# Skip term of five output sums moved from TensorE to ScalarE and GpSimd, last output sum in two halves

## The chip, the cores and the metric

One NeuronCore of a Trainium2 chip runs the whole program. The metric is device time in microseconds (us) of one execution. Before the change three runs took 287.53, 287.78 and 289.35 us, median 287.78 us. The profiled execution took 285.57 us, of which 283.8 us are the span from the first to the last instruction; the other 1.8 us lie around it.

## The reference

Two branches are computed from the same kind of input and blended by a gate for each token. Branch A is an attention with memory, 32 heads, in four segments of 512 tokens. Branch B is a state space convolution of the input, done as a long FFT, plus the input times a skip vector.

```
x = A_x
g = _sigmoid((x * gate_w).sum(-1, keepdims=True))
a = _A_ref(x, ...)          # heads' outputs o, then o @ wo
b = _B_ref(...)             # y, then y + u * Dskip
return g * a + (1 - g) * b
```

The output is 2048 x 512 in bf16. In the kernel the token is split as 16 p + b4, where p is a partition, so the output is made as 16 sums of 128 x 512, one for each b4 from 0 to 15. Every one of them is (1 - g) times a bracket of four parts: the attention output through wo (four 128-deep products, the factor g/(1 - g) put into the heads' outputs before), the convolution's two halves (one product each), and the skip term x * Dskip.

## The kernel before, in words

Nothing is scheduled while the program runs. Every operation is recorded by `op` with its engine and its dependencies; the table `ORDER` then fixes the order of all operations, the engine of those that either ScalarE or VectorE can do, and the slot of each buffer or PSUM bank. `replay` walks that table and `emit` writes five in-order instruction streams (PE, ACT, DVE, POOL, SP), where an instruction waits only on semaphores of what it depends on. All DMAs of the part that matters here are issued by SP, one behind the other: a DMA that waits for a buffer holds all DMAs behind it.

`conv` treats 32 units u. Names used below: `Ku` (a product on PE and its eviction), `Yu` (a product on VectorE), `Vu` (a product on PE, its eviction into a buffer of the pool V, and a DMA that spreads it into V2, whose second half V2[1] comes from units 16 to 31). The last units that run are 31, 29 and 30. `X31` is a DMA that Y31 needs.

`finals` makes the 16 sums, spread by `ORDER` over the last 35 us among the last attention and convolution work. For sum b4 the steps are named

- `fin`: first products into a PSUM bank; `fir`: convolution half 0 (V2[0]);
- `fih`: the last wo product, which needs the last heads (`oT3.3`); `fis`: convolution half 1, which needs V2[1] and so the DMAs of units 25, 26, 29 and 30;
- `out`: eviction times (1 - g), held in `omg4T`, then a 256 KB store for two sums together.

Sums 0 to 7 are *spilled* (`SPILL`): after `fir` the bank is emptied by `spl` on VectorE into an f32 buffer Ab and taken again by `fih`. Ab holds the skip term already: `xD` on VectorE (L1528) makes x times (1 - g) times Dskip, from x rows loaded by `xr` (L1524), two sums to a load. Sums 8 to 15 are *held*: they keep their bank from `fin` to `out`, and their skip term is made by PE, four 128-wide products of x transposed with a diagonal matrix, at the start of `fin` (L1534). Their `out` is a plain scaled copy, on ScalarE (L232) or VectorE (L233).

A bank that an eviction empties is given to a later product; the PE instruction waits for that eviction. In the program before, `fin0` takes the bank of `K30` and `fin14` the bank of `V29`.

Of the kernel before, what the change touches and what calls it, by code (L numbers as in the profile page):

```python
# [358 lines left out]
def c_pe(mode, *ns):  # L359
    return ("P", mode, ns)  # L360
# [14 lines left out]
NWARM = 5  # L375
SPILL = {0: 1, 1: 1, 2: 1, 3: 1, 4: 2, 5: 2, 6: 0, 7: 0}
# [89 lines left out]
1687/0/1 1688a 1742 840 1682/0 1683/4/0 1006/2 1007 1776 1689/3 1008 1724/2 1727 1702/0 1703 1718/6 1690/1/3 1719
1026/5 1027v 1764/2 1765 1766 1780/5 1732/1 1657 1684a 1740/0 1743 1797/4 1685 1798 1777 1691a 1692 1799 1704 1800/0
1801v 1767/1 1733/1 1753/1 1721/0 1778/2 1769/7 1717/3 1720 1712/4 1713/3 1714 1722/4 1723 1768a 1779a 1728/2 1729
1770 1781 1782 1783 1784a 1734/6 1771 1772 1773v 1802/3 1803 1804 1785 1774 1754/5 1755 1735 1737/4 1730 1760/0 1761
1736 1705/5 1706 1707 1744/7 1745/2 1786/1 1762 1731 1715 1763 1805 1806a 1807 1787 1788 1789/1 1746 1738 1739 1791/6  # L470
1792 1790a 1793 1794 1747 1795a 1796
# [70 lines left out]
def build_graph(nc, es, A_x, A_wq, A_wk, A_wv, A_wo, A_beta, B_A_re, B_A_im, B_B_re, B_B_im,  # L542
# [147 lines left out]
    xrP = mkpool("xr", 2048, 2, 3)  # L690
# [819 lines left out]
    def finals(V2, k0):  # L1510
# [4 lines left out]
        for b4 in range(16):  # L1515
            held = b4 not in SPILL
            S.key = k0 + b4
            P = S.ps()
            Ab = None if held else Tile(AbPs[SPILL[b4]], F32)
            if not held:  # L1520
                if b4 % 2 == 0:
# [4 lines left out]
                    xr[b4] = xr[b4 + 1] = T  # L1526
                S.tag = "xD%d" % b4
                op("DVE", ("V1s", 512), lambda e, b4=b4, Ab=Ab, T=xr[b4]: e.scalar_tensor_tensor(  # L1528
                    ap(Ab, n=512), ap(T, (b4 % 2) * 512, n=512), ap(omg4T, b4, n=1), ap(DbT, n=512), ALU.mult, ALU.mult), r=[xr[b4], omg4T, DbT], w=[Ab], key=k0 - 10 + b4)
# [126 lines left out]
```

## Time and profile before

| | |
|---|---|
| median of the runs | 287.78 us (287.53 to 289.35) |
| profiled execution | 285.57 us; span 283.8 us |
| PE busy | 258.8 us, 91% |
| DVE busy | 265.0 us, 93% |
| ACT busy | 254.3 us, 90% |
| POOL busy | 5.0 us, 2% (memsets at the start and two later) |
| granted TensorE clock | 0.993 over the span |

The page names the line of the helper that emits an instruction: L713 is every product of PE but a few, L229 and L230 are plain evictions on ACT and DVE, L232 and L233 scaled ones, L225 every DMA. The trace is followed in us from the start of the span. A row of the timeline has start, length, engine, line, operation, shapes, count, and in brackets the idle time of the engine ahead of it and what ended it.

### The profile page before, as it was taken

The page shows a single profiled execution, that of the slowest core. Times are in us where ns is not written, and L with a number is a line of the kernel's source. Part 1 is how long each engine was busy: PE and PEld are TensorE (multiplying, and loading weights), DVE is VectorE, ACT ScalarE, POOL GpSimd, SP SyncE. Part 2 cuts the span into 40 slices and gives each one's busy share as a digit, 9 for nine tenths or more (in the row PEclk, how much of TensorE's full clock was granted, in tenths as well). Part 3 has the DMA queues.
Part 4 walks back from the last instruction along what each step waited for, and adds up shares of the span by engine and source line. Part 5 has one row for each costly group of instructions (what it writes and reads, how often), then busy time and mean ns, then how long its engine had stood idle before and what let it go on. Part 6 is the DMA issues. An engine that isn't in the chain of part 4 may idle for free.

```text
span 283.8 us, 9330 instructions
## 1 busy us (share of the span) xinstructions
PE 258.8 (91%) x3947; PEld 157.5 (56%) x3947; DVE 265.0 (93%) x617; ACT 254.3 (90%) x320; POOL 5.0 (2%) x10
## 2 busy tenths in 40 slices
PE   5778888887989899989999989999999999999995
PEld 2434454564656556756765657665555454556663
DVE  3999999999999999999999999999999999997774
ACT  5999999999999999999989999999999999994122
POOL 5000000000000000000000000000000000000000
PEclk9999899999999999999999999999999999999999
DMA  6997752422115346824743388588676786793415
GB/s 164 274 203 173 218 170 85 130 80 53 42 28 143 76 114 183 229 86 73 214 135 103 76 254 236 183 207 203 207 223 171 217 192 187 219 206 105 116 74 222
DMA packets 60187, 44.49 MB, mean 157 GB/s; under 512 B 36209, under 2 KB 53490, under 8 KB 60146
## 3 DMA queue, kind: packets, MB, share of 16 engines
q1 hardware_dynamic: 60146, 43.90, 57.4%
q8 instruction: 31, 0.51, 0.8%
q14 instruction: 10, 0.08, 0.1%
HBM read 22.09 MB, written 7.86 MB: 106 GB/s over the span
## 4 chain that ended last, share of the span: by engine, by line
ACT 43%; PE 41%; DVE 9%; issue 4%; DMA 2%; SPq 0%; ACTq 0%; DVEq 0%
PE psum L713 40%; ACT sb L1197 15%; ACT sb L229 13%; ACT sb L1244 8%; DVE sb L1353 3%; ACT sb L857 3%; ACT sb L865 2%; DVE sb L1362 1%; DVE sb L1356 1%; DMA scr_Z<-sb 1%; ACT sb L1028 1%; DMA sb<-c_ident 1%; ACT sb L1079 1%; DVE sb L1365 1%; ACT L935 0%
## 5 line engine op out<-in xcount | busy, mean ns | idle before, releaser
L713 PE MATMUL psum<-sb 128*128 128x17 bf16 (+18 forms) x3859 | 253.2, 230 | 16.4 <-ACT sb L1197 7.4
L713 PEld LDWEIGHTS psum<-sb 128*128 128x128 bf16 (+6 forms) x3859 | 152.3, 101 | 115.1 <-issue 19.3
L229 ACT ACTIVATE sb<-psum 128x512 bf16<-128x512 f32 (+4 forms) x155 | 87.7, 624 | 6.5 <-PE psum L713 5.8
L1244 ACT ACTIVATE sb<-psum 128x2048 bf16<-128x2048 f32 x40 | 75.9, 1899 | 2.2 <-PE psum L713 1.8
L1197 ACT ACTIVATE sb<-psum 128x2048 bf16<-128x2048 f32 (+1 forms) x40 | 70.0, 1751 | 2.3 <-PE psum L713 2.1
L1353 DVE TENSOR_TENSOR sb<-sb 128x4096 bf16<-128x4096 bf16 (+3 forms) x24 | 37.6, 1567 | 0.0
L230 DVE CAST sb<-psum 128x512 bf16<-128x512 f32 (+1 forms) x49 | 29.9, 625 | 1.2 <-PE psum L713 0.9
L1362 DVE TENSOR_TENSOR sb<-sb 128x512 bf16<-128x512 bf16 (+1 forms) x48 | 24.9, 534 | 0.1
L1256 DVE TENSOR_TENSOR sb<-sb 128x1024 bf16<-128x1024 bf16 (+1 forms) x40 | 22.5, 576 | 0.2
L1494 DVE TENSOR_TENSOR sb<-sb 128x1024 bf16<-128x1024 bf16 x32 | 21.5, 684 | 0.9 <-ACT sb L229 0.5
L1356 DVE TENSOR_TENSOR sb<-sb 128x2048 bf16<-128x2048 bf16 (+3 forms) x24 | 20.6, 859 | 0.0
L232 ACT ACTIVATE sb<-psum,sb 128x512 bf16<-128x512 f32 x6 | 4.0, 687 | 12.3 <-PE psum L713 12.3
L1161 DVE TENSOR_TENSOR sb<-psum,sb 128x256 bf16<-128x256 f32 x32 | 13.3, 415 | 0.3
L1365 DVE TENSOR_TENSOR sb<-sb 128x512 bf16<-128x512 bf16 (+1 forms) x24 | 12.7, 531 | 0.0
L857 ACT ACTIVATE sb<-sb 128x512 f32<-128x512 f32 x18 | 11.8, 659 | 0.0
L1158 DVE RECIPROCAL sb<-psum 128x16 f32<-128x16 f32 x32 | 7.8, 249 | 2.0 <-PE psum L713 1.8
L1298 DVE TENSOR_TENSOR sb<-psum,sb 128x512 bf16<-128x512 f32 x12 | 8.3, 689 | 0.2
L865 ACT ACTIVATE sb<-sb 128x512 bf16<-128x512 f32 x12 | 8.0, 683 | 0.0
L1079 ACT ACTIVATE sb<-sb 128x512 bf16<-128x512 bf16 x12 | 8.0, 662 | 0.0
L1028 ACT ACTIVATE sb<-psum 128x512 bf16<-128x512 bf16 x12 | 7.7, 645 | 0.0
L858 DVE TENSOR_TENSOR sb<-sb 128x256 f32<-128x256 f32 x18 | 7.4, 418 | 0.0
L859 DVE SCALAR_TENSOR_TENSOR sb<-sb 128x256 f32<-128x256 f32 x18 | 7.4, 417 | 0.0
(78 smaller groups left out, 121.8 us busy)
## 6 DMA issues: line engine op xcount, KB each, us to landing
sb<-sb SPq DMA_DIRECT2D x64, 128.0 KB, 3.2
sb<-c_DN SPq DMA_DIRECT2D x32, 224.0 KB, 3.1
scr_Z<-sb SPq DMA_DIRECT2D x16, 256.0 KB, 2.7
sb<-scr_Z SPq DMA_DIRECT2D x16, 256.0 KB, 3.7
sb<-in_A_x_dram SPq DMA_DIRECT2D x5, 512.0 KB, 4.7
sb<-c_DN SPq DMA_DIRECT2D x16, 160.0 KB, 3.4
out_dram<-sb SPq DMA_DIRECT2D x8, 256.0 KB, 2.0
scr_O<-sb SPq DMA_DIRECT2D x12, 128.0 KB, 3.1
```

The lines of the kernel that those rows point to most:

```text
L229: fa = lambda e: e.activation(dst(), src(), ACT.Copy)
L230: fd = lambda e: e.tensor_copy(dst(), src())
L713: mm = lambda e, o_, l, r_, st, sp, **kw: e.matmul(o_, lhsT=l, rhs=r_, start=st, stop=sp, skip_group_check=True, **kw)
L857: op("ACT", ("As", 512), lambda e, sq=sq, Z=Z: e.activation(ap(sq, n=512), ap(Z, n=512), ACT.Square), r=[Z], w=[sq], key=PW[h] + PWS * k)
L1197: o = op("ACT", ("Ax", 4 * n), lambda e: e.activation(ap(pT, dims=[[512, 4], [1, n]]), ap(P, dims=[[512, 4], [1, n]]), ACT.Exp, scale=0.25 ...
L1244: o = op("ACT", ("Ax", 2048), lambda e, P=P, pT=pT: e.activation(ap(pT, n=2048), ap(P, n=2048), ACT.Exp, scale=0.25), r=[P], w=[pT])
L1256: op("DVE", ("V2", 128 * nb), lambda e, pT=pT, dims=dims: e.tensor_tensor(ap(pT, dims=dims + [[1, 128]]), ap(pT, dims=dims + [[1, 128]]), ...
L1353: op("DVE", ("V2n1" if n == 1 else "V2", 512 * n), lambda e: e.tensor_tensor(ap(tile, 2 * dst, [[2 * (sp - dst), 2], [2 * ne, 128], [1, 2 ...
L1356: op("DVE", ("V2n1" if n == 1 else "V2", 256 * n), lambda e: e.tensor_tensor(D_(), D_(), ap(tile, 2 * sp + ne * 128, [[-ne * 128, 2], [2 * ...
L1362: op("DVE", ("V2x" if sstep > 2 else "V2", 256 * n), lambda e, half=half: e.tensor_tensor(run(t2, n, 0, 1) if half else run(tile, ne, dst, ...
L1365: op("DVE", ("V2", 256 * n), lambda e: e.tensor_tensor(D_(), D_(), ap(t2, n * 128, [[-n * 128, 2], [2 * n, 64], [1, 2 * n]]), ALU.add), r= ...
L1494: op("DVE", ("V2", 1024), lambda e, Y=Y, XAB=XAB, K3=K3, Ke=Ke, xo=xo, u=u: e.tensor_tensor(ap(Y, dims=[[512, 2], [1, 512]]), ap(XAB, xo, ...
```

## The change

For five held sums, `DSK` = 9, 14, 8, 10 and 11, `fin` no longer makes the skip term on PE. It is made into an f32 buffer, as for a spilled sum, and `out` becomes an operation of VectorE that adds it while it evicts. For nine sums, `GSK` = those five and the spilled ones 2, 3, 4 and 5, the skip buffer is made in two steps: `xS` on ScalarE (x times 1 - g) and `xM` on GpSimd (times Dskip, in place). Sums 0, 1, 6 and 7 keep `xD` on VectorE. The five held sums load their x rows by five new DMAs of 128 KB, `xq`. GpSimd gets a library load (an instruction printed as ISA) ahead of its first product.

Sum 13, the last one, is made in two halves of 256 columns in two banks; its first half is evicted by ScalarE, its second by VectorE (`outb13`). Sums 12 and 13 are stored apart, 128 KB each.

```diff
+DSK = (9, 14, 8, 10, 11,)
+GSK = (3, 14, 5, 8, 10, 2, 9, 11, 4,)
...
-1686/0 1671 1009/5 1013 1696/2 1759 1622 1697/6/3 1698a 1699 1664 1005 1016 1017 1018 1019/1 1741/7 1020 1021/1
+1662/4/2 1663a 1686/0 1815/0 1734/1 1671 1009/5 1013 1696/2 1763 1622 1768/1 1816/0 1817 1785/2 1776/3 1697/6/3 1698a
...
-    xrP = mkpool("xr", 2048, 2, 3)
+    xrP = mkpool('xr', 2048, 4, 3)
+    xqP = mkpool('xq', 1024, 4, 3)
...
+    AbhP = mkpool('Abh', 2048, 6, 3)
...
+            skip = held and b4 not in DSK
...
+            last = b4 == 13
+            P = [S.ps(), S.ps()] if last else [S.ps()]
...
+            elif not skip:
+                S.tag = "xq%d" % b4
+                T, xo = Tile(xqP, BF16), 0
+                S.dma(lambda T=T: ap(T, n=512), lambda b4=b4: bass.AP(x.tensor, x.offset + b4 * 512, [[8192, 128], [1, 512]]), 131072, w=[T])
+            if not skip and b4 in GSK:
+                S.tag = "xS%d" % b4
+                op("ACT", ("As", 512), lambda e, b4=b4, Ab=Ab, T=T, xo=xo: e.activation(
+                    ap(Ab, n=512), ap(T, xo, n=512), ACT.Copy, scale=ap(omg4T, b4, n=1)), r=[T, omg4T], w=[Ab])
+                S.tag = "xM%d" % b4
+                op("POOL", ("G", 512), lambda e, Ab=Ab: e.tensor_tensor(
+                    ap(Ab, n=512), ap(Ab, n=512), ap(DbT, n=512), ALU.mult), r=[DbT], w=[Ab])
...
-                if held:
+            def f1(e, P=P, b4=b4, skip=skip):
+                w = 512 // len(P)
+                if skip:
                     for kc in range(4):
...
+                    op("PE", c_pe("F", 256, 256), f4, r=o4 + [woT, G2T, V2[1]], pw=[Pj], acq=[ou])
...
+                    S.evac(lambda ou=ou, j=j, b4=b4: ap(ou, (b4 % 2) * 512 + 256 * j, n=256), lambda Pj=Pj: ap(Pj, n=256), 256,
+                           r=[Pj, omg4T], pw=[ohs[j], ou], scale=lambda b4=b4: ap(omg4T, b4, n=1))
...
+            elif skip:
+                S.evac(dst, lambda P=P: ap(P, n=512), 512, r=[P, omg4T], pw=[ohs[0], ou], scale=lambda b4=b4: ap(omg4T, b4, n=1))
             else:
...
+            if b4 in (12, 13):
```

The order of PE's operations is the same before and after; `fin` of the five sums is shorter. The orders of SP and ACT differ.

SP, about 249 to 265 us of the trace. In the program before (the rows are, in order: oT1.3, V28, X31, xr2, CD30, V27, V20, V31 and V26, oT2.3, xr4, V25):

```order
L1309 DMA_TRANSPOSE sb<-scr_O 128x1x512
L225 DMA sb<-sb 8x16x512 [waits q_ACT]
L225 DMA sb<-sb 64x1024
L225 DMA sb<-in_A_x_dram 128x1024 [waits q_DVE]
L225 DMA sb<-c_DN 128x896 [waits q_PE]
L225 DMA sb<-sb 8x16x512 [waits q_ACT]
L225 DMA sb<-sb 8x16x512
L225 DMA sb<-sb 8x16x512 [waits q_ACT]
L225 DMA sb<-sb 8x16x512
L1309 DMA_TRANSPOSE sb<-scr_O 128x1x512
L225 DMA sb<-in_A_x_dram 128x1024
L225 DMA sb<-sb 8x16x512
```

And now (oT1.3, xr2, V28, X31, CD30, xq14, xr4, V27, V20, then xq8, xq10 and xq9 in one row, V31, V26):

```order
L1317 DMA_TRANSPOSE sb<-scr_O 128x1x512
L225 DMA sb<-in_A_x_dram 128x1024 [waits q_DVE]
L225 DMA sb<-sb 8x16x512 [waits q_ACT]
L225 DMA sb<-sb 64x1024
L225 DMA sb<-c_DN 128x896 [waits q_PE]
L225 DMA sb<-in_A_x_dram 128x512
L225 DMA sb<-in_A_x_dram 128x1024 [waits q_DVE]
L225 DMA sb<-sb 8x16x512 [waits q_ACT]
L225 DMA sb<-sb 8x16x512
L225 DMA sb<-in_A_x_dram 128x512 x3
L225 DMA sb<-sb 8x16x512 [waits q_ACT]
L225 DMA sb<-sb 8x16x512
```

xr2 stands ahead of V28 and X31 now, and xr4 ahead of V27; both wait for VectorE, xr2 for the end of xD1 and xr4 for the end of xD7, whose buffers they take (the order's slots of the pool xr are the same two as before, though it has four). xq11 is issued behind V30.

ACT, from the last exponentials (L1244 before, L1252 now) to its end. Before (V27, sc3.3.B1, then V26, V31, K30, V29, V30, then the evictions out8, out10, out11, out15, out12, out13):

```order
L229 ACTIVATE sb<-psum 128x512 x2
L1244 ACTIVATE sb<-psum 128x2048
L229 ACTIVATE sb<-psum 128x512 x5
L232 ACTIVATE sb<-psum,sb 128x512 x6
L1610 UNCONDITIONAL_BRANCH
```

And now (K29 and V27, sc3.3.B1, xS3, V26, xS14, V31, xS5 and xS8, K30, xS10, V29, xS2, V30, then xS9, xS4 and xS11, out15 and out12, half of out13):

```order
L1252 ACTIVATE sb<-psum 128x2048
L1545 ACTIVATE sb<-sb 128x512
L229 ACTIVATE sb<-psum 128x512
L1545 ACTIVATE sb<-sb 128x512
L229 ACTIVATE sb<-psum 128x512
L1545 ACTIVATE sb<-sb 128x512 x2
L229 ACTIVATE sb<-psum 128x512
L1545 ACTIVATE sb<-sb 128x512
L229 ACTIVATE sb<-psum 128x512
L1545 ACTIVATE sb<-sb 128x512
L229 ACTIVATE sb<-psum 128x512
L1545 ACTIVATE sb<-sb 128x512 x3
```

The five evictions of the convolution have six steps `xS` between and ahead of them, each of which waits for its x rows or stands behind one that does; ACT's eviction of V31 waits, before and after, for the DMA of V27, whose buffer it takes. out8, out10 and out11 have gone to VectorE.

GpSimd, from its last memset to its end, which had only the branch there before (xM3, 14, 5, 8, 10, 2, 9, 11 and 4 in this order; the last one waits for nothing that the one ahead had not waited for):

```order
L1003 MEMSET sb 128x128 [waits q_PE] x2
L1548 ISA
L1548 TENSOR_TENSOR sb<-sb 128x512 [waits q_ACT] x8
L1548 TENSOR_TENSOR sb<-sb 128x512
L1658 UNCONDITIONAL_BRANCH
```

VectorE loses xD3, xD5, xD4 and xD2 and gains out8, out10, out11 and the 256-wide outb13 at its very end.

More of the change, by code (lines that the diff above doesn't have):

```diff
@@ L466 @@
[L466 to L470, printed above, removed]
@@ L1546, in finals @@
             S.tag = "fir%d" % b4
[L1547 removed]
+            op("PE", c_pe("F", 512), lambda e, P=P, fv=fv, held=held: [fv(e, Pj, j, 512 // len(P), q=0, stop=not held) for j, Pj in enumerate(P)][-1], r=[G2T, V2[0]], pw=P)
             if not held:
                 S.tag = "spl%d" % b4
[L1550 to L1552 removed]
```

83 lines of the change are left out of this document (54 added, 29 removed).

## The prediction

> **What bounds the kernel now.** I read the chain of waits first, from the end.
>
> ```profile
> 248.28 32.26 PE psum L713 x261
> 280.53 0.02 issue
> 280.56 0.69 ACT sb L232
> ```
>
> The last 32 us before the final eviction are one unbroken run of TensorE products. The stretches of the trace say the same of the place where the sums are made (columns: stretch, length, busy time and count of PE, clock, DMA share, GB/s).
>
> ```profile
> 254.20:280.53 26.33, 26.32 (x213) 1.00 0.39 122
> 270.51:273.53 3.02, 3.02 (x15) 1.00 0.00 0
> 266.08:266.33 0.25, 0.25 (x5) 1.00 0.38 107
> ```
>
> PE has no gap to lose: whatever leaves its stream there comes off the end, unless a wait takes its place. The second row gives the pace of 512-wide products, 3.02 us for 14 that start in it, 0.216 us each. The third is the stretch from the start of fin11's four skip products to the start of its first wo product: 0.25 us for the four.
>
> VectorE is the next busiest; its evictions at the end:
>
> ```profile
> 268.95 0.75 DVE L233 TENSOR_SCALAR sb<-psum,sb 128x512 bf16<-128x512 f32 x1 [1.19 <-PE psum L713]
> 273.74 0.75 DVE L233 TENSOR_SCALAR sb<-psum,sb 128x512 bf16<-128x512 f32 x1 [0.61 <-PE psum L713]
> 275.28 1.41 DVE L1564 SCALAR_TENSOR_TENSOR sb<-psum,sb 128x512 bf16<-128x512 f32 x2 [0.80 <-PE psum L713]
> 277.27 2.72 DVE L1564 SCALAR_TENSOR_TENSOR sb<-psum,sb 128x512 bf16<-128x512 f32 x4
> ```
>
> It waits for PE three times, 2.6 us in all, and takes 0.66 us per operation back to back ((2.72 - 0.74) / 3). ScalarE has gaps among the convolution's evictions:
>
> ```profile
> 254.50 1.90 ACT L1244 ACTIVATE sb<-psum 128x2048 bf16<-128x2048 f32 x1
> 258.00 0.60 ACT L229 ACTIVATE sb<-psum 128x512 bf16<-128x512 f32 x1 [1.60 <-PE psum L713]
> 259.04 0.60 ACT L229 ACTIVATE sb<-psum 128x512 bf16<-128x512 f32 x1 [0.44 <-PE psum L713]
> 261.44 1.25 ACT L229 ACTIVATE sb<-psum 128x512 bf16<-128x512 f32 x2 [1.80 <-PE psum L713]
> 264.29 0.60 ACT L229 ACTIVATE sb<-psum 128x512 bf16<-128x512 f32 x1 [1.60 <-PE psum L713]
> ```
>
> These are sc3.3.B1, V26, V31, K30 with V29, and V30. But one of them is already what PE waits for:
>
> ```profile
> 262.08 0.42 PEld L713 LDWEIGHTS psum<-sb 128*128 128x128 bf16 x3 [0.32 <-ACT sb L229]
> ```
>
> That is fin0, whose bank K30's eviction (ended 262.04) sets free. A later K30 is a later PE.
>
> **The change part by part.** *Products removed.* Five times four skip products: 5 x 0.25 = 1.25 us, three quarters of a us of it between V30 and fis14 (fin8, fin11, fin14), one quarter before (fin10) and one behind (fin9).
>
> *SP.* The moved loads wait, and SP issues in order. What stood there:
>
> ```profile
> 251.12 1.21 SPq L225 DMA_DIRECT2D sb<-sb  x2
> 254.66 1.28 SPq L225 DMA_DIRECT2D sb<-sb  x2
> 262.15 0.58 SPq L225 DMA_DIRECT2D sb<-in_A_x_dram  x1
> 264.91 0.61 SPq L225 DMA_DIRECT2D sb<-sb  x1
> ```
>
> (V28 and X31; V27 and V20; xr4; V30.) And what the loads wait for, with what follows on VectorE:
>
> ```profile
> 250.53 1.41 DVE L1528 SCALAR_TENSOR_TENSOR sb<-sb 128x512 f32<-128x512 bf16 x2
> 255.69 0.75 DVE L1528 SCALAR_TENSOR_TENSOR sb<-sb 128x512 f32<-128x512 bf16 x1
> 256.35 0.69 DVE L1494 TENSOR_TENSOR sb<-sb 128x1024 bf16<-128x1024 bf16 x1
> ```
>
> xr2 now stands ahead of V28 and waits for xD1 to end, 251.94: V28 goes at 252.6 and not 251.12, X31 at 253.3 and not 251.8. Y31 (256.35) and what follows on VectorE come up to 1.0 us later, and PE, which takes up its results near 259, may lose the quarter of fin10 and 0.3 us more. That loss lies ahead of the next one and is not added to it.
>
> xr4 now stands ahead of V27 and waits for xD7 to end, 256.44. It takes 0.58 us to issue, so V27 goes at 257.06, 2.4 us later. ACT's eviction of V31 needs V27 landed. Times from issue to landing (last column), for 128 KB in the stretches 225 to 250, 240 to 250 and 250 to 262, for an x load at 262, and for the last store:
>
> ```profile
> sb<-sb SPq DMA_DIRECT2D x13, 128.0 KB, 3.1
> sb<-sb SPq DMA_DIRECT2D x5, 128.0 KB, 2.4
> sb<-sb SPq DMA_DIRECT2D x6, 128.0 KB, 4.1
> sb<-in_A_x_dram SPq DMA_DIRECT2D x1, 256.0 KB, 3.4
> out_dram<-sb SPq DMA_DIRECT2D x1, 256.0 KB, 2.0
> ```
>
> I take 3.1, the row with the most transfers, and keep 2.4 and 4.1 as bounds. V27 lands at 257.06 + 3.1 = 260.16. The rows for single steps:
>
> ```profile
> L1079 ACT ACTIVATE sb<-sb 128x512 bf16<-128x512 bf16 x12 | 8.0, 662 | 0.0
> ...
> L1528 DVE SCALAR_TENSOR_TENSOR sb<-sb x8: 742/745/751, 250.5 to 270.3; 128x512 f32<-128x512 bf16 x8
> ...
> L939 POOL MEMSET sb<- 128x544 f32 x1 | 0.9, 860 | 0.0
> ...
> L230 DVE CAST sb<-psum 128x512 bf16<-128x512 f32 x38 | 25.4, 685 | 1.2 <-PE psum L713 0.9
> L230 DVE CAST sb<-psum 128x256 bf16<-128x256 f32 x11 | 4.5, 417 | 0.0
> ```
>
> *ScalarE.* A step xS does what L1079 does, 0.66 us. V31's eviction runs 260.18 to 260.78, behind it xS5 to 261.44 and xS8 to 262.10 (xq8, issued about 258.3, landed at 261.4), and only then K30, to 262.70 and not 262.04. So fin0, and PE behind it, is 0.66 us later, with fin10's quarter gone too. xS10 and xS2 find room: V29 ends by 263.96, xS2 by 264.62.
>
> *Into fis14.* V30's eviction comes 0.66 later, at 264.95, its DMA at 265.57, landed 268.67. fis14 starts at 268.53 before (out14's 268.95 less one product of 0.38 and 0.04); without a wait it would start at 268.53 + 0.66 - 0.75 = 268.44. So it waits to about 268.70, 0.17 later than before. Behind it fin9's quarter counts: PE ends 0.08 earlier. With 2.4 us for a transfer, K30 is on time, V30 lands at 267.3, and PE ends 1.04 earlier; with 4.1 K30 is 1.66 late and V30 lands at 270.7, and PE ends 1.9 later.
>
> *VectorE* loses four xD and gains three evictions and half of one, 0.66 each. From out14 at 269.1, eight operations bring it to out9's end near 274.4; out6 can't start before PE's fis6, 275.2. It stays 0.8 ahead there, and 0.6 at outb13. The banks that its evictions free (out8's for fih3, spl2's for fin4) come 0.5 us in time. If that cover goes, its delay is PE's.
>
> *GpSimd* has shown no such product. Below: VectorE does it in 0.75. Above: a fill of 544 f32 takes 0.86, and two inputs and an output are at most three such passes, 2.6. I take two passes, 1.7, by the memset, the only row of the engine of this size. xM3 starts at 257.1; the eighth, xM11, ends at 257.1 + 8 x 1.7 = 270.7, wanted by out11 at about 273.1. Cost nothing. [...]
>
> *The end.* The last eviction was 0.69 us on ACT. In halves, the second one on VectorE is 0.27 us shorter than a full one (685 - 417 ns), so 0.75 - 0.27 = 0.48: 0.2 gained. Twice as many products of half the width in sum 13 have the same columns; I put 0.05 on it, 0 to 0.1. The last store moves half the bytes. What the DMA engines moved in 40 slices of the last 2.6 us:
>
> ```profile
> GB/s 284 410 410 441 347 378 158 32 0 0 0 0 0 63 252 378 473 410 284 378 441 441 347 347 189 32 0 0 0 0 0 0 0 0 0 0 0 0 0 0
> ```
>
> At the 400 or so of its middle 128 KB take 0.3, which I take; the bounds are 0 and half of the 2.0.
>
> Sum: -0.08 (PE) - 0.2 - 0.3 + 0.05 = -0.5 us. The profiled execution has 285.57 us (span 283.8), so 285.0; it lies 2.2 under the median of the runs, and I apply the difference to that: 287.78 - 0.5 = **287.2**. With the bounds of the transfers: -1.5 to +1.5.
>
> **Rivals.** *The full gain.* If x loads and V transfers land faster with xr4 out of the way at 262, K30 stays on time, V30 lands before PE comes, and all of it counts: -1.25 - 0.2 - 0.3 + 0.05 = -1.7, 286.1. For it speaks the 2.4 row; against it that xr4 can't go before 256.44, which is VectorE's row, not the transfers'. Chance 0.20.
>
> *The queue costs more.* With 4.1 us, the row of the stretch that begins at 250: +1.9 - 0.45, 289.2. Against it: that stretch carries transposes and convolution loads that are past by 257. Chance 0.10.
>
> *Slower by GpSimd.* One mechanism: xM11 is not there when VectorE, in order, comes to out11, and six evictions and the last half wait behind it. It decides from 257.1 + 8d > 273.9 (out11's turn and the 0.8 to spare), d over 2.1 us. At 2.6 xM11 ends at 277.9, 4.0 over; VectorE has 0.6 more to spare at the end, so 3.4 over the forecast: 290.6, slower than before by 1%. A late start counts as well: over 3.2 us more before the first product do it at d = 1.7. The order has a library load ahead of it; it is issued behind the last memset, with over 100 us to spare. For it: the engine's only rows are fills. Against: two passes stay under. Chance 0.08.
>
> [...]
>
> *Contention.* A GpSimd product and a VectorE operation may hold each other up where both read SBUF. Most of VectorE's work there reads PSUM and one buffer; Y30 reads two and stands between K30's eviction and V30's bank. It and the step behind it need 0.66 + 0.42 = 1.1 us of the 1.5 that PE's seven products from fin0 to V30 give them; held up by a whole product of 1.7, V30 and fis14 come 1.3 later. At half of that: -0.5 + 0.6, 287.9; at most 288.6. Chance 0.12. [...]
>
> **How the numbers follow.** Forecast 0.50, full gain 0.20, contention 0.12, more queue 0.10, GpSimd 0.08. The likeliest is 287.2. Low: the full gain 286.1 less 0.3, by which the two lower runs differ, 285.8. High: the queue's 289.2 less what leaves a part of it out, 289.0. One per cent, about what a measurement of this kernel tells from no change, is 2.9 us: no case reaches 284.9, so faster 0.02; only part of GpSimd's case reaches 290.7, so slower 0.05; the same 0.93.
>
> **What would show it.** Right: V27's DMA issued near 257.1 and V28's near 252.6; K30's eviction ending 0.5 or more later than 262.04 with xS8 just ahead of it; PE waiting for ACT before fin0 and for a DMA at fis14; the final eviction 256 wide and about 0.48 us; a GpSimd product under 2.1 us. Wrong: PE without a gap and ending 1.2 us earlier; out11 waiting for GpSimd; K30 on time although V27 is late; or Y29 and Y30 far over 0.69 us.

## The result, and the profile after

The changed kernel took 289.31 us (median of 22 runs, 286.26 to 291.61), the kernel before on the same chip 287.68 us (22 runs, 284.97 to 291.49). The ratio is 1.0054 with a 95% interval of 1.0030 to 1.0079: about 1.6 us slower (0.9 to 2.3). Runs that lie over 1.5% above their kernel's fastest are left out of the ratios, and the table further down gives the times with and without them. 287.2 was predicted, 0.6 us faster than before, with 289.0 as the upper end.

The profiled execution of the changed kernel took 288.43 us, its span is 286.6. Before the change reaches anything it is already 2.6 us behind: the granted clock was 0.50 in two stretches (from 20 to 22 us and from 34 to 38), in the profile of before in one (from 28 to 30). So the two spans can't be subtracted. I count the **tail** instead, from the start of ScalarE's eviction of V28, ahead of all that the change touches, to the issue of the last store. The two ends in the timeline of the kernel before (start, length, engine, line, operation):

```profile
250.50 0.59 ACT L229 ACTIVATE sb<-psum 128x512 bf16<-128x512 f32 x1
...
281.27 0.33 SPq L225 DMA_DIRECT2D out_dram<-sb  x1
```

And of the changed kernel:

```profile
253.14 0.59 ACT L229 ACTIVATE sb<-psum 128x512 bf16<-128x512 f32 x1
...
284.25 0.33 SPq L225 DMA_DIRECT2D out_dram<-sb  x1
```

30.77 us before, 31.11 now: 0.34 longer, where the forecast's step at the same place was 0.2 shorter (all but the store's landing). The chain of waits of the changed kernel is no longer one run of TensorE (start, length, what):

```profile
258.90 0.57 ACT sb L1545
259.47 3.85 DMA sb<-sb
...
263.40 0.60 ACT sb L229
264.00 0.87 ACT sb L1545 x2
...
265.12 0.59 ACT sb L229
...
265.76 2.18 PE psum L721 x9
...
267.96 0.60 ACT sb L229
...
268.59 3.31 DMA sb<-sb
...
271.94 7.33 PE psum L721 x36
```

This is the path that the prediction walked: V27's transfer, V31's eviction, the scalings xS5 and xS8, K30's eviction, fin0, V30's eviction and transfer, fis14. SP's timeline shows why V27 is late:

```profile
255.00 1.21 SPq L225 DMA_DIRECT2D sb<-sb  x2
...
256.87 2.55 SPq L225 DMA_DIRECT2D sb<-in_A_x_dram  x2
259.47 1.78 SPq L225 DMA_DIRECT2D sb<-sb  x2
```

V28 and X31 go 1.86 us behind V28's eviction, 0.62 before. Then xq14 and xr4 stand at the head for 2.55 us, and V27 goes at 6.33, 4.16 before: 2.17 later, 2.4 predicted. So far the reading holds. What it leaves out is in the groups of VectorE and GpSimd (from 245 us on; busy us, mean ns) and in their timeline:

```profile
L1548 POOL TENSOR_TENSOR sb<-sb 128x512 f32<-128x512 f32 x9 | 11.0, 1242 | 114.3 <-ACT sb L1545 114.3
L1576 DVE SCALAR_TENSOR_TENSOR sb<-psum,sb 128x512 f32<-128x512 f32 x8 | 5.9, 744 | 0.1
```

```profile
259.72 1.43 POOL L1548 TENSOR_TENSOR sb<-sb 128x512 f32<-128x512 f32 x1 [109.84 <-ACT sb L1545]
...
260.71 0.99 DVE L1264 TENSOR_TENSOR sb<-sb 128x1024 bf16<-128x1024 bf16 x1
```

On GpSimd the first multiplication, xM3, took 1.43 us and the fourth, xM8, 1.65; the others took 1.15 to 1.16. Beside xM3 VectorE's mask product mk3.3.B1 took 0.99 us, in before 0.68 (timeline of before):

```profile
257.61 0.68 DVE L1256 TENSOR_TENSOR sb<-sb 128x1024 bf16<-128x1024 bf16 x1
```

spl, which reads PSUM and one buffer, kept its 0.74.

### The profile page after: what moved, and what is told of

Same layout as the page of the kernel before. It is cut to its first block, busy times and chain, and to the rows that moved or that the text cites. A ratio compares the mean times of both kernels' runs of the same rounds, so it can differ in the third digit from the quotient of the medians.

```text
span 286.6 us, 9280 instructions
## 1 busy us (share of the span) xinstructions
PE 254.6 (89%) x3882; PEld 158.1 (55%) x3933; DVE 264.9 (92%) x617; ACT 258.1 (90%) x326; POOL 16.0 (6%) x19
## 4 chain that ended last, share of the span: by engine, by line
ACT 33%; PE 26%; DVE 24%; DMA 11%; issue 5%; SPq 0%; ACTq 0%; DVEq 0%
PE psum L721 25%; ACT sb L229 11%; ACT sb L1252 10%; ACT sb L1205 7%; DMA sb<-sb 5%; DVE sb L1361 5%; DVE sb L230 4%; DMA sb<-c_DN 3%; DVE sb L1370 2%; DVE sb L1502 2%; ACT sb L865 2%; DVE sb L1264 2%; DMA scr_Z<-sb 1%; DVE sb L1364 1%; DVE sb L1169 1%
## 5 line engine op out<-in xcount | busy, mean ns | idle before, releaser
L721 PE MATMUL psum<-sb 128*128 128x17 bf16 (+17 forms) x3794 | 249.0, 229 | 23.8 <-ACT sb L1205 7.3
L1252 ACT ACTIVATE sb<-psum 128x2048 bf16<-128x2048 f32 x40 | 75.9, 1897 | 2.5 <-PE psum L721 2.1
L1548 POOL TENSOR_TENSOR sb<-sb 128x512 f32<-128x512 f32 x9 | 11.0, 1242 | 114.3 <-ACT sb L1545 114.3
L1608 DVE SCALAR_TENSOR_TENSOR sb<-psum,sb 128x512 bf16<-128x512 f32 x13 | 8.9, 743 | 2.3 <-PE psum L721 2.3
L1003 POOL MEMSET sb<- 128x128 bf16 x4 | 2.5, 722 | 144.3 <-PE psum L721 144.3
L232 ACT ACTIVATE sb<-psum,sb 128x512 bf16<-128x512 f32 (+1 forms) x3 | 1.8, 616 | 9.3 <-PE psum L721 9.3
L1545 ACT ACTIVATE sb<-sb 128x512 f32<-128x512 bf16 x9 | 6.3, 718 | 2.3 <-DMA sb<-in_A_x_dram 2.3
```

The costliest lines, as they stand in the source:

```text
L721: mm = lambda e, o_, l, r_, st, sp, **kw: e.matmul(o_, lhsT=l, rhs=r_, start=st, stop=sp, skip_group_check=True, **kw)
L1252: o = op("ACT", ("Ax", 2048), lambda e, P=P, pT=pT: e.activation(ap(pT, n=2048), ap(P, n=2048), ACT.Exp, scale=0.25), r=[P], w=[pT])
```

## The experiments

All times below are us from the start of V28's eviction, from one profile each; an eviction or issue is told by its start. The last two columns are the time of a kernel's runs against those of before **at the same mean clock** (95% interval): over 357 runs of this study a mean clock lower by 0.001 went with 0.18 us more, and this is taken out. The second of them has only the runs that the ratios count, 280, where the slope is 0.12.

| kernel | V31 evicted | K30 evicted | oT3.3 evicted | V30 issued | tail | time, all runs | time, runs of the ratios |
|---|---|---|---|---|---|---|---|
| before | 8.54 | 10.94 | 14.45 | 14.41 | 30.77 | 0 | 0 |
| ctl_before (before) | 8.89 | 11.29 | 14.80 | 14.76 | 31.12 | in the row above | in the row above |
| halves | 8.55 | 10.94 | 14.46 | 14.42 | 30.58 | -0.7 (-1.3 to 0.0) | -0.3 (-0.8 to 0.3) |
| gp_only | 8.54 | 10.93 | 15.83 | 15.38 | 32.55 | +2.3 (1.4 to 3.2) | +2.0 (1.0 to 3.0) |
| changed | 10.26 | 11.98 | 15.61 | 15.44 | 31.11 | +1.0 (0.6 to 1.3) | +1.1 (0.8 to 1.5) |
| ctl_after2 (changed) | 9.49 | 12.91 | 17.12 | 17.08 | 32.39 | in the row above | in the row above |
| prod_back | 10.06 | 12.06 | 15.87 | 15.83 | 32.01 | +1.9 (1.2 to 2.6) | +1.8 (1.1 to 2.4) |
| nopool | 9.50 | 11.52 | 15.02 | 14.98 | 30.28 | -0.2 (-0.7 to 0.2) | -0.1 (-0.5 to 0.3) |
| nopool_again | 10.45 | 12.17 | 15.68 | 15.63 | 30.96 | in the row above | in the row above |
| slots | 9.23 | 11.95 | 15.52 | 15.48 | 30.77 | -0.2 (-0.9 to 0.4) | -1.0 (-1.7 to -0.2) |
| noxq | 8.80 | 11.19 | 15.32 | 15.28 | 30.56 | +0.5 (-0.3 to 1.3) | +1.2 (0.5 to 1.8) |
| act_only | 10.19 | 11.91 | 15.43 | 15.38 | 30.74 | -0.2 (-1.0 to 0.6) | -0.3 (-1.0 to 0.4) |
| all3 | 9.67 | 11.30 | 15.07 | 15.34 | 30.70 | -0.6 (-1.2 to 0.1) | -0.4 (-1.0 to 0.2) |
| best | 10.68 | 11.16 | 15.92 | 15.12 | 31.19 | +0.2 (-0.5 to 0.8) | +0.3 (-0.3 to 0.9) |
| best2 | 8.31 | 10.71 | 14.83 | 14.79 | 30.08 | -1.0 (-1.7 to -0.3) | -0.8 (-1.4 to -0.2) |
| best3 | 8.31 | 10.71 | 14.82 | 14.78 | 31.20 | +0.2 (-0.5 to 0.8) | +0.8 (0.2 to 1.3) |
| best4 | 8.31 | 10.76 | 14.27 | 14.23 | 29.54 | -0.9 (-1.4 to -0.5) | -0.4 (-0.8 to 0.0) |
| best4_again | 8.35 | 10.82 | 14.33 | 14.29 | 29.60 | in the row above | in the row above |

The two columns are 0.6 to 0.8 us apart for slots, noxq and best3, so these rows say least; the others are at most 0.5 apart. The runs were taken on several chips, each beside before; comparing within a chip only moves no row by more than 0.3.

The first expectations count from oT1.3's issue, which then moved by up to 0.94 us against ScalarE; hence the other mark. In the diffs the order's entries stand by name, a slot behind a stroke.

### The two kernels again

No edit.

> The kernel before, unchanged, as a run of its own beside the others, so that its clock is known run by run. The tail is counted here and below from the issue of the last transposing transfer of column 1 (oT1.3, which the change leaves alone) to the issue of the last store: 31.78 us in the profile of before. Theory Q (queue and eviction order: the change loses its gain in the tail alone): tail 31.6 to 31.9 us again, ratio 0.998 to 1.002. Theory C (the changed program draws more half-clock stretches ahead of the tail, and that is most of the loss): mean clock of these runs above that of the changed kernel by 0.004 or more.

Ratio 1.0017 (0.9979 to 1.0056), tail 31.12 us: 0.35 more than in the first profile of the same kernel, and there already where the last long exponentials but one start (sc3.3.A1, 1.63 behind V28's eviction, 1.27 in the first profile). That is how far one profile's tail can be trusted.

> The changed kernel again, on the same chip as the three others. Theory Q: tail 32.1 us as in its profile (+0.3 against before), time 0.1 to 0.6 us above before at the same clock. Theory C: same tail, time 1 to 2 us above before, with a mean clock lower by 0.004 or more.

Ratio 1.0018 (0.9972 to 1.0065). The granted clock dropped within this tail (0.98 from 264.1 to 267.3 us, 1.00 from 254 to 260; 0.988 over the profile), so its 33.1 us can't be used. Theory C gets half an answer: over all its 46 runs the changed kernel's mean clock was 0.9832, before's 0.9862 (163 runs). That is worth 0.5 us and makes the 1.0 us at the same clock into the 1.5 measured.

### The slots of xr2 and xr4

```diff
-xr2/0 ... xr4/1
+xr2/2 ... xr4/3
```

> The changed kernel with the two loads xr2 and xr4 put into slots 2 and 3 of their pool, which lie unused, so that neither waits for a product of VectorE (xD1, xD7) at the head of SP's queue. Nothing else is changed. Theory Q: V27's transfer is issued right behind its eviction, 2.2 us earlier against oT1.3 than in the changed kernel; V31's eviction comes 0.9 to 1.7 us earlier, K30's 0.7 to 1.0 us earlier, and the tail is 31.3 to 31.7 us (0.4 to 0.8 shorter than that of the changed kernel). Rival X (what holds K30's eviction are the two scalings xS5 and xS8 ahead of it on ScalarE, not the queue): K30's eviction moves by 0.3 us at most and the tail stays within 0.2 us of 32.1. Theory C: times stay 1 us or more above before whatever the tail does.

V27 goes at 4.24 and no longer waits, V31's eviction comes 1.0 us earlier, but K30's not at all (11.95). By oT1.3's mark the tail is 31.78, just outside the 31.3 to 31.7. Ratio 0.9984 (0.9936 to 1.0033). The chain names what K30 waits for now:

```profile
257.30 5.72 DMA sb<-in_A_x_dram
263.02 0.02 issue
263.04 0.36 ACT sb L1545
```

The load of xq8 took 5.72 us, and xS8 waited for it at ScalarE's head with K30's eviction behind. Both readings were half right: the wait on SP went, and ScalarE's order took its place.

### SP's and ScalarE's order, first try

Against the slots run:

```diff
 SP:  xr2/2 V28 X31 CD30
-xq14 xr4/3 V27 V20 xq8
+V27 V20 xq14 xr4/3 xq8
 ACT: V31
-xS5 xS8 K30 xS10 V29
+K30 xS5 xS8 xS10 V29
```

> As the run before it, and moreover V27's and V20's transfers go ahead of the loads xq14 and xr4 on SP, and K30's eviction goes ahead of the scalings xS5 and xS8 on ScalarE. Theory Q: nothing that the change added stands ahead of the chain V27, V31, K30, V30 any more; K30's eviction is within 0.2 us of before against oT1.3, V30's transfer too, and the tail is 30.6 to 31.3 us, since 1.25 us of products less is all that is left of the change: time 0.5 to 1.2 us below before. Rival X: the same tail, but the run before it has not shortened. Rival G (GpSimd's products slow VectorE and ScalarE down, whatever the order): tail at 31.7 or more, with evictions and masks of 0.9 to 1.0 us where before has 0.6 to 0.7. Theory C: time within 0.3 us of the changed kernel's.

K30 is 0.36 us late, where at most 0.2 was expected, and V29 and V30 now stand behind scalings (chain of waits):

```profile
265.08 0.71 ACT sb L1545
265.79 0.48 ACT sb L229
266.28 0.61 ACT sb L1545
266.89 0.49 ACT sb L229
```

V30's transfer is 0.93 late. The tail by oT1.3's mark, 31.72, is outside the expected 30.6 to 31.3. Ratio 0.9997 (0.9959 to 1.0035): theory Q's gain of 0.5 to 1.2 us doesn't appear there, and at the same clock the gain of 0.4 to 0.6 us can't be told from none.

### All evictions ahead of the scalings but two

Against the run before:

```diff
 SP:
-xr2/2 V28 X31 CD30 V27
+V28 X31 xr2/2 CD30 V27
 ACT: V31
-K30 xS5 xS8 xS10 V29 xS2 V30
+K30 V29 xS5 xS8 V30 xS10 xS2
```

> The changed kernel with slots 2 and 3 for xr2 and xr4, with V28's, X31's, V27's and V20's transfers issued on SP ahead of the loads that the change put before them, and with the evictions of K30, V29 and V30 put ahead of the scalings on ScalarE (xS5 and xS8 behind V29's eviction, xS10 and xS2 behind V30's). Tails are counted from oT1.3's issue to the last store's issue: before 31.78 and 31.83, changed 32.11, with the slots alone 31.78, with the first reordering 31.72. Theory Q2 (V30's transfer sets the end: it was issued 1.03 us later in the changed kernel, 1.08 with slots alone, 0.94 with the reordering, because V29's eviction still stood behind three scalings and V30's behind a fourth; from its landing to the last store it is 1.1 us less than before in all of them): V30's transfer within 0.2 us of before (15.4 to 15.7 us behind oT1.3), tail 30.6 to 31.0. Rival G (GpSimd's and VectorE's interference, whatever the order): V30's transfer at 16.2 or later, tail 31.5 or more.

V30's eviction came at 14.0, but the tail is 31.19 us: worse. Ratio 1.0003 (0.9964 to 1.0043). xS14 had stayed ahead of V31's eviction (timeline of ScalarE):

```profile
262.18 0.72 ACT L1545 ACTIVATE sb<-sb 128x512 f32<-128x512 bf16 x1 [2.05 <-DMA sb<-in_A_x_dram]
262.81 1.55 ACT L229 ACTIVATE sb<-psum 128x512 bf16<-128x512 f32 x3
```

It waited 2.05 us for xq14. With V31's eviction, oT2.3's transfer stands back in SP's queue, and that was the path which the prediction had not seen (chain of waits):

```profile
264.73 3.23 DMA sb<-scr_O
...
268.05 0.70 DVE sb L230
...
268.80 9.54 PE psum L721 x46
```

oT2.3 lands, oT3.3 is evicted, fih8 and all behind it follow. Two paths run from V31's eviction, one by V30's transfer and one by oT2.3's. In the changed kernel V30 lands at 18.75, and oT3.3's eviction ends at 16.30 with ten products of 0.216 us to come ahead of fis14: 18.46, an estimate, only 0.3 sooner. V27's transfer also took 4.67 us to land here, against 2.97 in before and 3.53 in all3 (all profiles at the end).

### The parts alone

The halves on the kernel before:

```diff
+fin13 into two banks, out13 on ACT and outb13 on DVE, st12 apart (nothing else of the change)
```

> The kernel before with only the last part of the change: the sum of block 13 in two halves of two banks, evicted by ScalarE and VectorE, and blocks 12 and 13 stored apart. No skip term is made elsewhere, no load is moved. The prediction had 0.2 us for the earlier last eviction and 0.3 us for the smaller store, less 0.05 for the split: tail 31.5 to 31.65, and the last store 1.7 us from issue to landing in place of 2.0. Rival (the two halves cost the engines what they save): tail 31.75 or more. The profile of the changed kernel had 1.91 us from the last store's issue to its landing, so 0.1 us less of the store's time is what is expected now.

0.19 us off the tail, ratio 1.0001 (0.9961 to 1.0042). The mark by oT1.3 gives 31.22 as that transfer itself went 0.37 late. The last store of the changed kernel took 1.91 us to land, 2.00 before: 0.1, where 0.3 was predicted.

GpSimd's multiplications left out of the changed kernel:

```diff
-xM3 xM14 xM5 xM8 xM10 xM2 xM9 xM11 xM4
```

> The changed kernel with the nine multiplications on GpSimd left out: the skip terms made by ScalarE then lack the factor by columns, everything else is in place and in order. Theory Q2: what the change loses, it loses by SP's and ScalarE's order, so the tail is 31.8 to 32.2 us, at most 0.3 us below that of the changed kernel (32.11), and V30's transfer is issued 16.0 to 16.5 us behind oT1.3. Rival G (interference): mask product and Y products at 0.68 to 0.70 us throughout instead of 0.99, 1.2 and more, V30's transfer at 15.6 or earlier and the tail at 31.4 or below.

V31's eviction came 0.77 us earlier here, by the landings, so the shorter tail alone decides little; the durations do (timeline of VectorE: mk3.3.B1, Y29, Y30):

```profile
261.23 0.68 DVE L1263 TENSOR_TENSOR sb<-sb 128x1024 bf16<-128x1024 bf16 x1
...
263.42 0.68 DVE L1501 TENSOR_TENSOR sb<-sb 128x1024 bf16<-128x1024 bf16 x1
...
265.25 0.69 DVE L1501 TENSOR_TENSOR sb<-sb 128x1024 bf16<-128x1024 bf16 x1 [0.77 <-ACT sb L229]
```

Ratio 0.9973 (0.9934 to 1.0011). Theory Q2 expected at most 0.3 us off and got 0.8; rival G had the tail right and V30's place not.

The five groups of products put back into it:

```diff
-skip = held and b4 not in DSK   (in f1)
+skip = held                     (in f1)
```

> The changed kernel with the five groups of four products on TensorE put back (the skip term is then counted twice in those five blocks), everything else as it is. Theory Q2: the four groups ahead of fis14 (1.0 us) lie in time in which TensorE waits for K30's and V30's evictions and V30's transfer, so they cost nothing there, and only the group of block 9 (0.25 us) shows: tail 32.3 to 32.5 us. Rival P (TensorE's work sets the end): all 1.25 us come back, tail 33.2 to 33.5.

The tail is 0.90 us longer than in the first profile of the changed kernel, but shorter than in ctl_after2 (32.39). By the times it is 0.9 longer (0.2 to 1.7), in the runs of the ratios 0.6 (-0.1 to 1.3); ratio to before 1.0053 (1.0004 to 1.0102). By oT1.3's mark the tail is 33.02, between theory Q2's range and rival P's. One stretch decides it, since it hardly varies: from oT3.3's eviction to the last store's issue. It has 16.12 us in halves and 16.14 here, with the products, and 15.25 to 15.31 in eleven profiles without them (the other three: 15.50 in the changed kernel's first and 15.63 in all3, both held by V30's transfer, and 16.38 in best3, held by GpSimd). So the removed products, 1.25 us of TensorE's time, were worth 0.8 to 0.9 there, far more than theory Q2's 0.25: with oT3.3's path as late as V30's, the products between fih8 and fis14 count too.

### Loads, ScalarE, and both

The slots run without the xq loads:

```diff
-T, xo = Tile(xqP, BF16), 0 ; S.dma(... xq ...)
+T, xo = xr[0], 0            (slots of xr2 and xr4: 2 and 3)
```

> Tails are counted from here on from ScalarE's eviction of V28 to the issue of the last store, since oT1.3's own issue moved by up to 0.94 us against the evictions in two runs: before 30.77, changed 31.11, slots alone 30.77, TensorE's products put back 32.01. This kernel is the one with slots 2 and 3 and without the five xq loads: the scalings of blocks 14, 8, 10, 9, 11 read the first loaded block in their place (their skip term is then that of another block), so nothing else moves. Theory L (traffic: V27's transfer of 128 KB landed in 3.0 us before, 3.9 to 5.7 us in the runs where the loads stand beside it, and ScalarE's scalings wait for the loads): V27 lands within 3.6 us, V31's eviction is at most 8.9 us behind V28's (before 8.54, slots 9.23), tail 30.2 to 30.5 us. Rival: the loads' traffic is harmless and xr2 with xr4 make the delay: V31's eviction at 9.2 or later, tail 30.7 or more.

V31's eviction at 8.80, of which 0.43 is a later sc3.3.A1 that the loads have no part in: no later than before. V27 landed in 3.34 us, in the slots run in 4.90, so V31's delay there came with the loads, as far as one profile each can tell. The tail is 30.56, a little over what was expected; ratio 1.0045 (0.9998 to 1.0093). Why the time of these eight runs is above before while the tail is below stays open.

ScalarE's order alone, against the changed kernel:

```diff
 ACT:
-xS3 V26 xS14 V31 xS5 xS8 K30 xS10 V29 xS2 V30
+V26 V31 xS3 xS14 K30 V29 xS5 xS8 V30 xS10 xS2
```

> The changed kernel with ScalarE's order alone put right: xS3 and xS14 behind V31's eviction, xS5 and xS8 behind V29's, xS10 and xS2 behind V30's; SP's queue as the change has it. If the evictions are late by ScalarE's order, V31's eviction is at 9.0 to 9.3 us behind V28's (changed 10.26) and the tail 30.2 to 30.5 us. If they are late since V27 is issued 2.17 us later on SP (6.33 in place of 4.16 behind V28's eviction): V31's eviction stays at 9.5 to 10.3, K30's comes right behind it (10.9 to 11.5), tail 30.5 to 31.1 us.

The second case: V31 stays at 10.19, so SP's queue is what holds it. K30, at 11.91, is later than the 11.5 expected: xS3 and xS14 now stand between the two. Tail 30.74, ratio 0.9959 (0.9916 to 1.0003).

Both orders:

```diff
 SP:  as in best
 ACT: as in act_only
```

> ScalarE's order as in the run before and SP's with slots 2 and 3, the transfers of V28, X31, V27 and V20 ahead of xr2, xq14 and xr4; all loads still stand directly behind V20's transfer. Theory L: V27's transfer shares the DMA engines with four loads and lands in 4.0 to 4.8 us, V31's eviction at 9.3 to 10.0 us, tail 30.2 to 30.7. If order is all that matters: V31's eviction at 8.6 to 8.8, oT3.3's at 14.4 to 14.6, tail 29.6 to 29.9.

V31's eviction at 8.31 and K30's at 10.71, ahead of before, although V27 took 3.83 us to land: with the order right, a landing of that length did no harm here, against theory L. Ratio 0.9953 (0.9908 to 0.9999). But V29 and V30 are 0.4 us late, and the timelines of GpSimd and VectorE say why:

```profile
262.89 2.72 POOL L1548 TENSOR_TENSOR sb<-sb 128x512 f32<-128x512 f32 x2 [113.84 <-ACT sb L1545]
...
263.05 1.55 DVE L1502 TENSOR_TENSOR sb<-sb 128x1024 bf16<-128x1024 bf16 x1
```

Y29 began 0.16 us behind xM3 and took 1.55 us in place of 0.68.

The loads thinned out:

```diff
 SP:  as in best2, but xr4 behind oT2.3, xq8 behind V29, xq10 and xq9 behind V30
 ACT: xS14 behind V29; xS5 xS8 xS2 xS10 behind V30
 DVE:
-spl5 spl0
+spl0 spl5
```

> As the run before, and the loads thinned out: only xq14 directly behind V20's transfer, xr4 behind oT2.3's, xq8 behind V29's, xq10, xq9 and xq11 behind V30's; the scaling of xS14 goes behind V29's eviction and all others but xS3 behind V30's, and spl5 behind spl0 on VectorE. Theory L: V27 lands in 3.0 to 3.6 us, V31's eviction at 8.5 to 8.9, oT3.3's at 14.3 to 14.9 and V30's transfer at 14.3 to 14.7; what the change saves is then left, 0.2 us of the halves and up to 0.9 of the products: tail 29.7 to 30.2 us, time 0.6 to 1.1 us below before at the same clock. Rival G (the products of GpSimd, now 2 us later, hold the evictions of blocks 14, 8, 10, 9, 11): tail 30.4 or more, with VectorE's out8, out10 and spl2 waiting for GpSimd.

V27 landed in 3.90 us with fewer loads beside it, not in theory L's 3.0 to 3.6. Y29 met xM3 again (1.55 us), so V30's transfer is no earlier than in best2. And rival G's second form came true. Tail 31.20, ratio 1.0035 (0.9994 to 1.0077), and VectorE waits for GpSimd (waits, us in total, times, longest):

```profile
DVE sb L1608 <- POOL sb L1548: 1.0, 1, 1.0
DVE sb L1576 <- POOL sb L1548: 0.8, 1, 0.8
```

Nine multiplications of 1.16 us needed an early start here.

### GpSimd alone, and kept apart

Nine multiplications in the kernel before, behind xr2:

```diff
+for j in range(9):   # when xr2 has landed, on buffers nobody reads
+    op("POOL", ("G", 512), lambda e, G=G: e.tensor_tensor(
+        ap(G, n=512), ap(G, n=512), ap(DbT, n=512), ALU.mult), r=[DbT, T], w=[G])
```

> The kernel before with nothing but nine multiplications of GpSimd put in, of the changed kernel's form, on tiles that nothing else reads, started by the landing of xr2 and running one behind the other from about 5.9 to 16.4 us behind V28's eviction. Theory G: mask product mk3.3.B1, Y29 and Y30 of VectorE take 0.99 to 1.6 us each in place of 0.68, V30's eviction comes 0.5 to 1.5 us later than in before (13.79) and the tail is 31.2 to 32.3 us (before 30.77). If they don't meet on the path: tail within 0.2 us of before. A cost that comes with GpSimd's first use, outside the tail, would show as time above before by more than the tail is longer.

The kernel before with these nine is 1.8 us longer in the tail, a little over the expected range, and 2.3 us (1.4 to 3.2) by the times of its six runs; ratio 1.0119 (1.0030 to 1.0207). Nothing waits for their results. No cost outside the tail is to be seen. Timeline:

```profile
257.44 13.02 POOL L1534 TENSOR_TENSOR sb<-sb 128x512 f32<-128x512 f32 x9 [108.49 <-DMA sb<-in_A_x_dram]
...
261.05 0.85 DVE L1162 TENSOR_TENSOR sb<-sb 128x16 f32<-128x16 f32 x1
...
262.27 1.25 DVE L1497 TENSOR_TENSOR sb<-sb 128x1024 bf16<-128x1024 bf16 x1
...
265.44 1.31 DVE L1537 SCALAR_TENSOR_TENSOR sb<-sb 128x512 f32<-128x512 bf16 x1
```

A division step of 16 columns took 0.85 us, Y29 1.25, xD3 1.31 in place of 0.74.

> The changed kernel once more. Its undisturbed profile had a tail of 31.11 us (0.34 above before), but its times lie 0.9 us above before at the same clock (interval 0.5 to 1.3). If the profile caught a short tail, this one is 31.3 to 31.8 us; if the profile is typical, 31.0 to 31.2 and the rest lies ahead of the tail or was chance, and the time at the same clock is 0.2 to 0.6 us above before.

No edit. The first profile had been a mild one: there mk3.3.B1 lost 0.31 us and a division step 0.07, and nothing else. Here X31 landed later, and VectorE's steps met GpSimd's one after another (timelines):

```profile
260.96 1.16 POOL L1548 TENSOR_TENSOR sb<-sb 128x512 f32<-128x512 f32 x1 [109.18 <-ACT sb L1545]
263.12 1.15 POOL L1548 TENSOR_TENSOR sb<-sb 128x512 f32<-128x512 f32 x1 [1.01 <-ACT sb L1545]
...
261.51 1.15 DVE L1502 TENSOR_TENSOR sb<-sb 128x1024 bf16<-128x1024 bf16 x1 [1.20 <-DMA sb<-sb]
...
263.25 1.57 DVE L1264 TENSOR_TENSOR sb<-sb 128x1024 bf16<-128x1024 bf16 x1
```

Y31 0.47 us longer, mk3.3.B1 0.89, and further down a division step 0.4 and Y29 0.57: 2.3 us. The tail is 32.39, 1.6 above before; the mean of both profiles is +1.0, as the times at the same clock say. In ctl_after's profile, whose tail can't be used, the same four steps lost 0.60, 0.71, 0.77 and 0.57 us, 2.6 together (its timeline, without Y29):

```profile
257.23 1.29 DVE L1502 TENSOR_TENSOR sb<-sb 128x1024 bf16<-128x1024 bf16 x1 [1.07 <-DMA sb<-sb]
...
259.10 1.39 DVE L1264 TENSOR_TENSOR sb<-sb 128x1024 bf16<-128x1024 bf16 x1
...
261.46 0.95 DVE L1167 TENSOR_TENSOR sb<-sb 128x16 f32<-128x16 f32 x1
```

Ratio 1.0058 (1.0023 to 1.0093).

The multiplications moved away from Y29 and Y30:

```diff
 SP:  as in best2
 ACT: as in best2, but
-sc3.3.B1 V26 V31 xS3 xS14 K30 V29 xS5 xS8 V30
+sc3.3.B1 xS3 V26 V31 K30 V29 xS14 xS5 V30 xS8
```

> Counted from V28's eviction. As best2, with four entries moved on ScalarE: xS3 ahead of V26's eviction, so that GpSimd's xM3 runs at about 7.6 to 8.8 us and not beside VectorE's Y29 (9.8 us), and xS14 behind V29's eviction with xS5, the others behind V30's, so that no multiplication of GpSimd runs beside Y29 or Y30. Theory G (a multiplication of GpSimd and a product of VectorE slow each other: in best2 Y29 took 1.55 us in place of 0.68, and V29's and V30's evictions are 0.4 us later for it than in before): Y29 and Y30 at 0.68 to 0.70, V29's eviction at 11.5 to 11.7, V30's at 13.7 to 13.9, oT3.3's at 14.3 to 14.6, tail 29.6 to 29.8 us (best2 30.08, before 30.77), time 0.7 to 1.4 us below before at the same clock. Rival: the 0.4 us have another cause (V20's late landing at 8.8 us), and V30's eviction stays at 14.1 to 14.2 with the tail at 30.0 to 30.1.

Y29 and Y30 took 0.68 and 0.69 (mk3.3.B1 still met xM3 and took 1.18), V30's transfer is issued 0.18 us ahead of before, and TensorE is one run again from 253.4 to the end (chain of waits):

```profile
253.43 31.23 PE psum L721 x247
284.66 0.02 issue
284.68 0.48 DVE sb L233
```

Tail 29.54, 1.23 below before and 1.6 below the changed kernel's first profile. The ratio of the runs doesn't show it, 1.0027 (0.9990 to 1.0063): their mean clock was 0.9832.

> The version that keeps GpSimd's multiplications away from Y29 and Y30, once more. Its tail was 29.54 us (1.23 below before), but its runs had a mean clock of 0.9832 (before 0.9866) and a median 0.4 us above before. If the gain of the tail reaches the time and the clock was chance: tail 29.4 to 29.9, mean clock 0.985 to 0.990, time 0.6 to 1.3 us below before. If kernels with GpSimd's multiplications draw a lower clock (148 runs of such kernels so far: 0.9841, 162 without: 0.9870): clock again 0.984 or below, time within 0.5 us of before.

Tail 29.60, mean clock 0.9866, ratio 0.9991 (0.9943 to 1.0039), median 286.48 against 288.35. At the same clock both series give -0.9 us (-1.4 to -0.5). By the tails and at the same clock this version beats both kernels. The plain ratios show no difference from before, and over their runs alone the comparison at the same clock has -0.4 (-0.8 to 0.0): against the changed kernel the gain is clear, against before its size is open.

> The changed kernel without GpSimd's nine multiplications (the skip terms made by ScalarE lack the factor by columns), once more: its tail was 30.28 us, against 31.11 and 32.39 for the changed kernel with them, and the mean clock of its 10 runs was 0.9914. If the interference is the larger part of the loss: tail 30.1 to 30.6 again, with mk3.3.B1, Y29, Y30 at 0.68 to 0.70 us, and time 1.0 to 2.0 us below the changed kernel's at the same clock. If the first profile was a lucky draw of the landings: tail 30.8 or more. Mean clock: 0.987 or more if GpSimd's work lowers it, else near 0.984.

V31 came late this time, so the tail is 30.96, over the 30.8 that was set for a lucky first draw: part of the first 0.8 us was luck. It is only 0.15 below the changed kernel's first profile, which had V31 about as late and in which the multiplications cost VectorE 0.4. Over both, nopool's tails are 30.6 on average, the changed kernel's 31.75, and the times at the same clock are 1.2 us apart (0.7 to 1.8; over the runs of the ratios the same). Ratio 1.0005 (0.9968 to 1.0043). The mean clock of its 22 runs was 0.9885. All kernels with the multiplications have 0.9843 (160 runs), all without 0.9865 (197); the difference, 0.0023 with a standard error of 0.0009, is 0.4 us. Whether the multiplications lower the clock stays open: in the changed kernel's first profile both stretches at 0.50 lie ahead of 40 us, the first multiplication begins at 259.72, and from 45 us on the granted clock is 1.00.

## Why the prediction was wrong

The forecast was -0.5 us, the outcome +1.0 at the same clock. **The step that failed is "GpSimd ... Cost nothing".** It asked only whether the products are ready in time, and they were, at 1.16 us each rather than 1.7. What they cost is VectorE's time while they run: 1.2 us in the changed kernel (0.7 to 1.8, nopool), 2.3 where they stand alone in before (1.4 to 3.2, gp_only). One profile can hide it: VectorE's steps lost 0.4 us in the first of the changed kernel and 2.6 and 2.3 in the two later ones.

The rival **contention** named this mechanism, but placed it at Y30 alone, at half a product, with a chance of 0.12. All of Y31, mk3.3.B1, the division steps and Y29 read two buffers as well, and lost up to 0.6 us (Y31 in ctl_after), 0.9 (mk3.3.B1 in ctl_after2, Y29 in best2) and 0.77 (a division step in ctl_after) in the timelines above. The rows for counting them were there: a list of VectorE's `sb<-sb` forms between 256 and 264 us would have given five exposed steps beside Y30 (these three and two division steps). The rival's upper end, 288.6, is 0.8 us above before's median, the outcome at the same clock 1.0.

**SP.** V28 1.24 us later (1.5 predicted), V27 2.17 (2.4): right. Its landing, "I take 3.1", was 3.85 in the first profile but 3.28 and 3.08 in the two later ones: near enough. K30 came 1.04 us late in place of 0.66, the first eviction behind fis14 (out14) 0.77 late, where fis14 was to be 0.17 late. "That loss lies ahead of the next one and is not added to it", on Y31, was wrong too: Y31 was 0.45 and 1.29 us late in the two profiles, and a late Y31 is what meets xM3.

**ScalarE.** The order of xS5, xS8 and K30 was read rightly, 0.60 to 0.66 us each in a row. That a scaling also waits for its own load at the head (2.05 us in best) was in the text on the order, not in the sum.

**Products removed.** The sum has 1.25 gained by them and 1.17 lost by the queue and the order, -0.08 together. They were worth about 0.9, and the path by oT3.3, which the prediction doesn't mention, was as late as the one by V30.

**The end.** -0.2 for the eviction was right (0.19 off the tail); -0.3 for the store was 0.1.

**Slower by GpSimd.** xM11 was never awaited in the changed kernel. In best3, where most of the products start 4 to 5 us later, VectorE waited for GpSimd twice, 1.0 and 0.8 us.

**The signs.** All those set for "right" came: V27's and V28's places, K30 behind xS8, PE's waits for ScalarE (0.8 us) and a DMA (0.5), the final eviction of 0.48 us, products under 2.1 us. So they were no test of the sum. Of those set for "wrong" only the last came, and only in the later profiles (Y29 1.25).

The parts, as an estimate: products -0.9, halves -0.2, interference +1.2, and what is left of +1.0 is +0.9 for the queue, the order and the loads together. Products and queue cancel nearly as forecast, both about 0.3 smaller, which is partly luck; the interference is what the sum lacked. The slots run, 1.2 us below the changed kernel at the same clock (0.5 to 1.9), fits that; over the runs of the ratios it is 2.1 (1.3 to 2.9), so the queue's share is the least certain.

## What to carry to other kernels

An engine with time to spare was not free here: GpSimd's nine multiplications cost 1.2 us in the changed kernel (nopool) and 2.3 in the kernel before (gp_only). So before work goes to GpSimd, list VectorE's instructions with two SBUF sources in the stretch where it will run: here one of them took up to 0.89 us longer beside a multiplication of 1.15 (mk3.3.B1 in ctl_after2, 1.57 in place of 0.68). spl and out, which read PSUM and one buffer, kept their 0.74 to 0.75, so such work is best put beside them. And a load or a scaling put ahead of an eviction in an in-order queue cost its own wait as well as its length: behind xr4 V27's transfer went 2.17 us later, and in best xS14 held ScalarE for a wait of 2.05 us and its own 0.72. Evictions on the path go first.

## What the runs showed of the hardware

The first thing is the interference of VectorE and GpSimd. In 14 profiles there are 24 cases where a product of VectorE with two SBUF sources (Y, mk, xD) began while a multiplication of GpSimd ran and was drawn out: each ended 0.545 to 0.551 us behind GpSimd's end, whenever it had begun (in ctl_after2 mk3.3.B1 ended at 264.82, the multiplication at 264.27). In the 16 cases where GpSimd's began behind VectorE's and was drawn out, it ended 1.01 to 1.03 us behind VectorE's end (in the changed kernel xM3 at 261.15, Y31 at 260.13); undisturbed it takes 1.15 to 1.18. In four more the two began within 0.04 us of each other, GpSimd's no later, and GpSimd's was the one drawn out. spl and out, with one source in PSUM, kept 0.74 to 0.75 us throughout.

The second thing is how much the landing of one and the same 128 KB transfer between SBUF buffers varies. V27 took 2.64 to 3.60 us in the four profiles without the new loads (before, ctl_before, halves, gp_only), 3.34 in noxq, and 3.08 to 4.90 in the fourteen with them; the same order of SP's first loads gave 3.83, 3.22 and 3.24 (best2, best4, best4_again). The two longest, 4.90 in slots and 4.67 in best, suggest that the loads beside it delay it. That isn't shown, since the ranges overlap and the loads stood ahead of it as well as behind.
